# Two buffers of scaled q and k, gathered rows by DMA, some squares off ScalarE, and the FFN in steps: a cosine-attention and mixture-of-depths kernel

## The chip, the cores and the metric

The kernel runs on one core of a Trainium2 chip. Five engines work on queues of their own: TensorE (PE, with PEld for its weight loads), VectorE (DVE), ScalarE (ACT), GpSimd (POOL) and SyncE (SP), the last of which here only issues DMAs. The metric is device time in microseconds (us). Before the change the median of three runs was 270.01 us (269.08 to 270.80).

## The reference

Two stages, the second on the output of the first. Shapes: q, k, v are (8, 12, 448, 64) float32, that is 8 batches, 12 heads, 448 tokens, 64 columns per head.

```python
# attention, for each batch and head
q_n = q / (norm(q) + 1e-6);  k_n = k / (norm(k) + 1e-6)
attn = softmax(q_n @ k_n.T / tau)          # tau = 0.1
x = concat over heads of (attn @ v)        # (8, 448, 768)
# mixture of depths, for each batch
scores = x @ w_gate                        # one number for each token
top_idx = the 128 tokens with the highest score
xe = x[top_idx]
ye = relu(xe @ w1) @ w2                    # 768 -> 1024 -> 768
out = x;  out[top_idx] = xe + sigmoid(scores[top_idx])[:, None] * ye
```

## The kernel before

**Slots.** Two heads make a pair; there are 48 pairs, six for each batch. The main loop runs over 48 slots, and slot `i` is the turn of pair `i`. In it the kernel computes the pair's scores in four pieces (`scores`, L275 and L280; three pieces hold both heads' 128 keys, the fourth, "piece 3", the 64 keys left over of each head), takes their exponentials on ACT (`exps`, L288 and L291), and multiplies the exponentials of the pair before by the values (`pv_tails` L304, `pv` L315). `pv_evac` (L331, L333) divides by the softmax sum on DVE and writes 128 columns of the batch's float32 tile `x_b`.

**What a slot prepares for later ones.** The squares of q and k of pair `i+5` are taken on ACT (`square`, L187); PE adds them up by eight matmuls with the identity (`sum_pe`, L194), DVE finishes the sum (L202), and for one or two pairs at a time (`NORMS`) ACT takes the logarithm and the exponential (L210, L211), POOL adds 1e-6 (L217) and DVE inverts (L220). POOL multiplies q and k of pair `i+2` by this (`scale`, L230, into the one tile `qkn`) and casts the values (`values`, L237). PE transposes the scaled q and k of pair `i+1` in 28 small transposes (`transposes`, L257), and DVE copies the result out of PSUM (`qkT_copy`, L263). POOL casts the new columns of `x_b` to bf16 (`half_x`, L354, tile `xh`).

**Mixture of depths.** The work for batch `b` is put into the slots after its last pair, counted from slot `s = 6*(b+1)`, by a table (`late`, `mid`, `early`, `last`) and the helpers `at` and `run`; a letter in the table names a place inside the slot. In order: `store_x` writes the whole `x_b` to `out` (two DMAs on SP, L346 and L347), `gate` computes the scores on DVE (L361), `rank_prep` (POOL, L371 to L374) and `rank_rep` (PE, L392, L396) spread them over partitions, `rank_count` (DVE, L416) counts how many tokens score higher, `pick` (L424) makes a 0/1 matrix, `select` (L433, L436 to L440) reads the row indices and gates out of it, and `gather` (L473) multiplies `xh` by the 0/1 matrix on PE, 24 matmuls for a batch, which gives the chosen rows already transposed; DVE copies them (L457). `ffn1` (L491, twice 24 matmuls) and `ffn2` (L500, twice 8 wide matmuls) follow, one call in one place of one slot each; their results are taken out of PSUM by DVE or ACT (L455, L459, L461). `scatter` (L515) is an indirect DMA from POOL that adds the rows of `oe` onto `out`.

**Order.** It is written out by hand: each engine works through its own queue in program order, and waits are on semaphores. In a slot PE's order is: score piece 0, tails, sums, `pv`, piece 3, piece 1, transposes, piece 2, and at place "B" the FFN step. Two PSUM buffers hold score pieces, and the sums of squares share the one of piece 3, so piece 1 waits for the exponential of piece 0, piece 2 for that of piece 3, and piece 0 of the next slot for that of piece 1. SP's queue holds all loads of q, k and v (`load`, L98 and L108, four groups of up to three pairs ahead) and the stores; POOL's queue holds the loads of the two weight matrices and the scatters. Every access to `out` is kept in order with the earlier ones that may overlap it; a scatter counts as touching the whole of `out`.

**The end.** After slot 47 the last batch has no later slots to hide in: x of pair 47, the gate of its last columns, rank, pick, gather, FFN and scatter follow one another, with the FFN of batch 6 between. For the last batch the chosen rows of x are read back by an indirect DMA (L711) from a copy `x_copy` that SP writes beside `out`, and the last scatter (L726) writes plainly.

Of the kernel before, what the change touches and what calls it, by code (L numbers as in the profile page):

```python
# [14 lines left out]


@with_exitstack
def kernel(
# [18 lines left out]
    P = 128  # L37
# [44 lines left out]
    NORMS = [(0, 1), (1, 2), (3, 1), (4, 1)]  # L82
    while sum(NORMS[-1]) < N:
        NORMS.append((sum(NORMS[-1]), min(2, N - sum(NORMS[-1]))))
# [56 lines left out]
    kn = const.tile([P, 2, NB7, Dh], BF16, name="qkn")  # L141
# [11 lines left out]
    tokc = const.tile([P, NS, 2], BF16)  # L153
    for half in range(2):
        for col, base, step, mult in ((0, 0, 0, 4), (1, NC * half, 1, 3)):
            nc.gpsimd.iota(tokc[half * T:half * T + T, :, col], pattern=[[step, NS]],
                           base=base, channel_multiplier=mult,
                           allow_small_or_imprecise_dtypes=True)
# [23 lines left out]
    ss_tiles, rs_tiles, sq_tiles = {}, {}, {}  # L182

    def square(p):
        gi, g = place[p]
        sq_tiles[p] = prep.tile([P, 2, NB7 * Dh], BF16, name="sq", bufs=3)
        nc.scalar.activation(  # L187
            sq_tiles[p], raw[gi % NRAW][0][:, :, g].rearrange("p a b d -> p a (b d)"),
            AF.Square)
# [8 lines left out]
    def sum_dve(p, dst):  # L198
        n, m = nplace[p]
        if m == 0:  # L200
            ss_tiles[n] = prep.tile([P, 2, 2, NB7], FP32, name="ss")
        nc.vector.tensor_reduce(  # L202
            ss_tiles[n][:, m].rearrange("p a b -> p (a b)"),
            dst.rearrange("p (n d) -> p n d", d=D8), axis=AX.X, op=ALU.add)

    def norm_a(n):
        gn = NORMS[n][1]
        rs = prep.tile([P, 2, 2, NB7], FP32, name="rs", bufs=3)
        rs_tiles[n] = rs
        nc.scalar.activation(rs[:, :gn], ss_tiles[n][:, :gn], AF.Ln)  # L210
        nc.scalar.activation(rs[:, :gn], rs[:, :gn], AF.Exp, scale=0.5)  # L211
# [7 lines left out]
    def norm_c(n):  # L219
        nc.vector.reciprocal(norm_of(n), norm_of(n))  # L220

    def scale(p, split=False):
        gi, g = place[p]
        qk = raw[gi % NRAW][0]
        n, m = nplace[p]
        rs = rs_tiles[n]
        parts = (((nc.gpsimd, 0, NC), (nc.vector, NC, NB7)) if split
                 else ((nc.gpsimd, 0, NB7),))
        for eng, b0, b1 in parts:
            eng.tensor_mul(  # L230
                kn[:, :, b0:b1], qk[:, :, g, b0:b1],
# [19 lines left out]
    def transposes(p):  # L251
        for a in range(2):
            for s in range(NB7):
                for u in range(2):
                    r = slice(u * T, u * T + T)
                    o = column(a, u, s)
                    nc.tensor.transpose(out=qkT_ps[r, o:o + T], in_=kn[r, a, s],  # L257
# [51 lines left out]
    def pv(i):  # L309
        ex = exp_tiles[i]  # L310
        vo = vo_bufs[i % NB]
        for u in range(2):
            for j in range(NS):
                for c in range(NC):
# [34 lines left out]
    def half_x(i):  # L349
        b, hp = divmod(i, HP)  # L350
        if hp == 0:
            xh_tiles[b] = xp.tile([P, NS, D], BF16, name="xh", bufs=3)
# [14 lines left out]
    def rank_prep(b, eng=nc.gpsimd):  # L367
        g = gates[b % 2]
        sg = moe.tile([P, NS, 3], BF16, name="sg")
# [58 lines left out]
    def select(b):  # L428
        sel, sg = st[b]["sel"], st[b]["sg"]
        pk = bank()  # L430
        for o, w, src in ((0, 2, tokc), (2, 3, sg)):
            for j in range(NS):
                nc.tensor.matmul(out=pk[:, o:o + w], lhsT=sel[:, j], rhs=src[:, j],  # L433
                                 start=(j == 0), stop=(j == NS - 1))
        gr = moe.tile([P, 1], FP32, name="gr")
        nc.vector.tensor_reduce(gr, pk[:, 2:5], axis=AX.X, op=ALU.add)  # L436
# [3 lines left out]
        nc.vector.tensor_scalar_add(idx, pks, float(b * S))  # L440
        st[b].update(idx=idx, gr=gr)
# [36 lines left out]


    def ffn1(b, part, eng="D", big=False, cut=0, between=None):  # L480
        xeT = st[b]["xeT"]
        h = moe.tile([P, 4, CAP], BF16, name=f"hT{part}")
        st[b].setdefault("hT", []).extend(h[:, t] for t in range(4))
        ps = bank(big)
        order = [(f, t) for t0, t1 in ((0, cut), (cut, KD)) for f in range(4)
                 for t in range(t0, t1)]
        for m, (f, t) in enumerate(order):
            fc = part * 4 + f
            if between and m == len(order) // 2:
                between()  # L490
            nc.tensor.matmul(out=ps[:, f * CAP:(f + 1) * CAP],  # L491
                             lhsT=w1_sb[:, t, fc * P:(fc + 1) * P],
                             rhs=xeT[t], start=(m == 0) if cut else (t == 0),
                             stop=(t == KD - 1), skip_group_check=bool(cut))
        evac(eng, h.rearrange("p t c -> p (t c)"), ps, AF.Relu)
# [7 lines left out]

    def ffn2_evac(b, n, ps, eng):
        if n == 0:
            st[b]["oe"] = moe.tile([P, D], FP32, name="oe")
        evac(eng, st[b]["oe"][:, n * ND:(n + 1) * ND], ps[:, :ND], AF.Copy, st[b]["gr"])

    def ffn2(b, n, eng="D", big=False):
        ps = bank(big)  # L510
        ffn2_mm(b, n, ps, 0, KF)
        ffn2_evac(b, n, ps, eng)

    def scatter(b):
# [3 lines left out]
            in_=st[b]["oe"][:CAP], in_offset=None, compute_op=ALU.add)  # L518
# [7 lines left out]
    def run(slot, where):  # L526
        for fn, args in work.pop((slot, where), []):
# [3 lines left out]
    late = dict(gate=((2, "D1"), (3, "D1"), (4, "D1"), (5, "D1")), rep=5, rank=6, select=7,  # L531
                ffn=((8, "B"), (9, "B"), (10, "B"), (11, "A")))
    mid = dict(late, ffn=((8, "B"), (9, "AA"), (9, "B"), (10, "A")))
    early = dict(gate=((2, "D1"), (3, "D1"), (3, "D1"), (4, "D1")), rep=4, rank=5,
                 select=6, ffn=((7, "B"), (8, "AA"), (8, "B"), (9, "A")))
    last = dict(gate=((1, "D1"), (2, "D1"), (2, "D1"), (3, "D1")), rep=3, rank=4,
                select=5, ffn=())
    for b in range(B - 1):
        s = HP * (b + 1)
        m = last if b == B - 2 else early if b == B - 3 else mid if b == B - 4 else late  # L540
        at(s, "P2", store_x, b)
        for j in range(NS):
            d, w = m["gate"][j]
            at(s + d, w, gate, b, j)
        at(s + m["gate"][3][0], "P1b", rank_prep, b)
        at(s + m["rep"], "B", rank_rep, b)
        for j in range(NS):
            at(s + m["rank"], ("D0", "D1", "D3", "D3")[j], rank_count, b, j)
        for j in range(NS):
            at(s + m["rank"], "D3", pick, b, j)  # L550
        at(s + m["select"], "A", select, b)
        at(s + m["select"], "C", select_b, b)
        at(s + m["select"], "B", gather, b, 0, "A" if b == B - 2 else "D")
        if b < B - 2:
            at(s + m["select"] + 1, "A", gather, b, 1)
        for (d, w), (fn, n) in zip(m["ffn"], ((ffn1, 0), (ffn1, 1), (ffn2, 0), (ffn2, 1))):
            at(s + d, w[0], fn, b, n, "A" if w == "AA" else "D")
            if fn is ffn2 and n == 1:
                at(s + d + 1, "P2", scatter, b)
    bb = B - 1  # L560
    gc = const.tile([P, NS], FP32)

    for j in range(NS):
        at(N - 1, "P2", gate, bb, j, 0, 5 * P, None, gc)
    at(N - 1, "P2", store_x, bb, None, 0, 5 * P)
    at(N - 1, "P2", store_x, bb, None, 0, 5 * P, x_copy)
    at(5, "D1", load_wg)
    at(7, "P2", load_w, w1_sb, moe_w1, kn[:, 1, 0, 0:1])
    at(10, "P2", load_w, w2_sb, moe_w2, kn[:, 1, 0, 0:1])

    SQ = {}
    for p in range(3, N):
        SQ.setdefault({3: 0, 4: 1, 5: 1, 6: 2}.get(p, p - 5), []).append(p)
# [34 lines left out]
    due = []  # L608
    for i in range(N + 1):
        live, prev, nxt = i < N, i > 0, i + 1 < N  # L610
# [6 lines left out]
        run(i, "P1")  # L617
        sq = SQ.get(i - 1, [])
        scores(i, 0)
        if prev:  # L620
            pv_tails(i - 1)
        exps(i, 0)
        for p in SQ.get(i, []) if i else []:
# [140 lines left out]
```

## Time and profile before

| | |
|---|---|
| median of three runs | 270.01 us |
| the profiled execution's own time | 268.42 us |
| its span, first to last instruction | 266.6 us |
| ACT busy | 203.3 us (76%) |
| PE busy | 225.2 us (84%) |
| DVE busy | 175.2 us (66%) |
| POOL busy | 168.3 us (63%) |
| granted TensorE clock | 0.985 |
| moved by DMA | 53.18 MB |

The time of an execution is 1.8 us longer than its span. A busy PE isn't PE at its peak, since matmuls overlap in the pipeline; what counts is whether one group of matmuls starts where the one before it lets it. The slots can be marked off by the exponential of piece 3 (L291), which each slot has once: it starts at 12.43 us in slot 0, at 62.86 us in slot 11, 68.86 us in slot 12 and 237.14 us in slot 47. The six slots from 23 to 28 take 28.4 us.

### The profile page before, as it was taken

What the parts mean: (1) busy time and instruction counts of PE and PEld (TensorE: products, weight loads), DVE (VectorE), ACT (ScalarE), POOL (GpSimd) and SP (SyncE); (2) the same over time, 40 slices, a digit from 0 to 9 for tenths busy, and PEclk for the clock granted to TensorE, in tenths of its full rate; (3) what the DMA queues carried; (4) which work ended last, traced back from release to release, by engine and by line L of the source; (5) the groups of instructions that cost most, each with busy time, mean ns of one, the idle gap of its engine ahead of it and who ended that gap; (6) DMA issues with size and microseconds to landing.
All of it is one profiled execution on the core that took longest, in us unless ns stands there. A gap on an engine that the chain in (4) does not pass through costs nothing.

```text
span 266.6 us, 10588 instructions
## 1 busy us (share of the span) xinstructions
PE 225.2 (84%) x4584; PEld 169.9 (64%) x4584; DVE 175.2 (66%) x472; ACT 203.3 (76%) x322; POOL 168.3 (63%) x234
## 2 busy tenths in 40 slices
PE   7678877586899979999899979998999899989920
PEld 6456655465678557767677757866786667757810
DVE  2424445474977778858877778678876976898401
ACT  3698999897897798888888789779878986683400
POOL 5367676979766568575966667757846885743131
PEclk9999999999999999999999999999999999999995
DMA  7999999999999974799679985999580049047861
GB/s 248 285 286 279 264 254 275 368 260 259 267 285 350 235 161 64 167 276 285 130 153 262 260 203 84 216 283 274 101 192 20 2 61 210 4 61 161 255 116 63
DMA packets 32431, 53.18 MB, mean 199 GB/s; under 512 B 2176, under 2 KB 28672, under 8 KB 31488
## 3 DMA queue, kind: packets, MB, share of 16 engines
q1 hardware_dynamic: 28976, 45.13, 63.9%
q0 software_dynamic: 2992, 6.69, 14.6%
q8 instruction: 36, 0.59, 1.0%
q10 hardware_dynamic: 416, 0.69, 0.7%
q14 instruction: 11, 0.09, 0.1%
HBM read 40.11 MB, written 15.53 MB: 209 GB/s over the span
## 4 chain that ended last, share of the span: by engine, by line
PE 35%; DMA 21%; DVE 16%; ACT 12%; issue 7%; SPq 4%; POOL 3%; POOLq 1%; ACTq 0%
DMA v_raw<-in_v_dram 11%; PE m_ps L491 7%; ACT expS L288 7%; PE m_ps L500 6%; PE sc L275 6%; PE o_ps L315 5%; DVE junk L416 4%; DVE junk L361 3%; DMA qk_raw<-in_k_dram 3%; DMA qk_raw<-in_q_dram 3%; PE sc L194 3%; ACT expS L291 3%; PE qkT_ps L257 3%; DVE xeT L457 2%; DVE x_b L333 2%
## 5 line engine op out<-in xcount | busy, mean ns | idle before, releaser
L288 ACT ACTIVATE expS<-sc 128x896 bf16<-128x896 f32 x144 | 125.3, 917 | 17.0 <-PE sc L275 16.4
L230 POOL TENSOR_TENSOR qkn<-qk_raw,rs 128x896 bf16<-128x896 f32 (+1 forms) x48 | 80.3, 1673 | 36.4 <-PE qkT_ps L257 26.3
L275 PE MATMUL sc<-qkT 64*128 64x448 bf16 x288 | 52.3, 358 | 14.8 <-DVE qkT L263 7.3
L187 ACT ACTIVATE sq<-qk_raw 128x896 bf16<-128x896 f32 x48 | 45.2, 947 | 2.1 <-DMA qk_raw<-in_k_dram 2.0
L315 PE MATMUL o_ps<-vo,expS 128*128 128x65 bf16 x1152 | 44.6, 193 | 1.5 <-issue 1.5
L315 PEld LDWEIGHTS <-expS 128*128 128x128 bf16 x1152 | 40.3, 97 | 2.1 <-issue 1.7
L275 PEld LDWEIGHTS <-qkT 64*128 64x128 bf16 x288 | 15.4, 92 | 37.3 <-issue 21.0
L263 DVE COPY qkT<-qkT_ps 128x960 bf16<-128x960 bf16 x48 | 31.3, 653 | 7.8 <-PE qkT_ps L257 6.8
L291 ACT ACTIVATE expS<-sc 128x448 bf16<-128x448 f32 x48 | 25.7, 536 | 13.3 <-PE sc L280 13.2
L333 DVE TENSOR_TENSOR x_b<-o_ps,rden 128x512 f32<-128x512 f32 x47 | 32.5, 691 | 1.6
L257 PEld LDWEIGHTS <-qkn 64*64 64x64 bf16 x1344 | 24.9, 109 | 12.9 <-issue 8.4
L257 PE MATMUL qkT_ps<-iden_b,qkn 64*64 64x64 bf16 x1344 | 30.4, 194 | 3.2 <-POOL qkn L230 2.1
L354 POOL CAST xh<-x_b 128x512 bf16<-128x512 f32 x47 | 29.7, 633 | 2.0 <-DVE gr L436 1.3
L361 DVE CUSTOM_DVE_ANT_0 junk<-x_b,wg_b 128x768 bf16<-128x768 f32 (+1 forms) x32 | 30.5, 953 | 0.5 <-DMA wg_b<-in_moe_w_gate_dram 0.3
L194 PE MATMUL sc<-sq,iden_b 128*128 128x112 bf16 x384 | 26.9, 215 | 2.4 <-ACT expS L288 2.3
L202 DVE TENSOR_REDUCE ss<-sc 128x14 f32<-128x112 f32 x48 | 12.8, 273 | 24.4 <-PE sc L194 24.0
L237 POOL CAST vo<-v_raw 128x448 bf16<-128x448 f32 x48 | 26.8, 557 | 0.8 <-DMA v_raw<-in_v_dram 0.7
L217 POOL TENSOR_SCALAR rs<-rs 128x28 f32<-128x28 f32 (+1 forms) x26 | 8.0, 307 | 25.8 <-ACT rs L211 21.7
L491 PEld LDWEIGHTS <-w_sb 128*128 128x128 bf16 x384 | 22.2, 98 | 3.3 <-issue 3.1
L194 PEld LDWEIGHTS <-iden_b 128*128 128x128 bf16 x384 | 20.8, 98 | 4.6 <-issue 1.7
L416 DVE SCALAR_TENSOR_TENSOR junk<-m_ps,own,tie 128x448 bf16<-128x448 f32 (+1 forms) x28 | 19.0, 678 | 0.5
L491 PE MATMUL m_ps<-xeT,w_sb 128*128 128x128 bf16 x288 | 18.1, 219 | 1.3 <-DVE xeT L457 1.3
(90 smaller groups left out, 275.6 us busy)
## 6 DMA issues: line engine op xcount, KB each, us to landing
qk_raw<-in_q_dram SPq DMA_DIRECT2D x15, 672.0 KB, 10.1
qk_raw<-in_k_dram SPq DMA_DIRECT2D x15, 672.0 KB, 12.0
v_raw<-in_v_dram SPq DMA_DIRECT2D x30, 192.0 KB, 9.6
out_dram<-x_b SPq DMA_DIRECT2D x7, 768.0 KB, 7.8
v_raw<-in_v_dram SPq DMA_DIRECT2D x30, 144.0 KB, 9.0
out_dram<-x_b SPq DMA_DIRECT2D x7, 576.0 KB, 4.7
w_sb<-in_moe_w_dram POOLq DMA_DIRECT2D x2, 1536.0 KB, 18.9
out_dram<-x_b SPq DMA_DIRECT2D x1, 640.0 KB, 6.7
```

Of the source, the lines that this page charges most:

```text
L187: nc.scalar.activation(sq_tiles[p], raw[gi % NRAW][0][:, :, g].rearrange("p a b d -> p a (b d)"), AF.Square)
L194: nc.tensor.matmul(out=dst, lhsT=iden_b, rhs=sq[:, :, s * D8:(s + 1) * D8], start=(s == 0), stop=(s == Dh // D8 - 1))
L230: eng.tensor_mul(kn[:, :, b0:b1], qk[:, :, g, b0:b1], rs[:, m, :, b0:b1].rearrange("p a (b o) -> p a b o", o=1) .to_broadcast([P, 2, b1 - ...
L257: nc.tensor.transpose(out=qkT_ps[r, o:o + T], in_=kn[r, a, s], identity=iden_b[r, r], tile_position=(u * T, u * T))
L263: nc.vector.tensor_copy(qkT_tiles[p], qkT_ps[:, :W])
L275: nc.tensor.matmul(out=sc[:, u, :S], lhsT=qkT[r, KO + c * P:KO + (c + 1) * P], rhs=qkT[r, :S], start=True, stop=True, tile_position=(u * D ...
L288: nc.scalar.activation(ex[:, 2 * c:2 * c + 2], sc[:, :, :S], AF.Exp, scale=inv_tau)
L291: nc.scalar.activation(ex[:, TAIL], sc[:, 0, :S], AF.Exp, scale=inv_tau)
L315: nc.tensor.matmul(out=o_ps[:, u, j * E:(j + 1) * E], lhsT=ex[:, 2 * c + u, qc(j)], rhs=vo[:, u * NS + c], start=False, stop=(c == NC - 1) ...
L333: nc.vector.tensor_mul(dst.rearrange("p j (u d) -> p j u d", u=2), o[:, :, :, :Dh], rden.to_broadcast([P, NS, 2, Dh]))
L361: nc.vector.tensor_tensor_reduce(out=junk[:, d0:d1], in0=src, in1=wg_b[:, d0:d1], scale=1.0, scalar=0.0 if prev is None else prev[:, j:j + 1],
L491: nc.tensor.matmul(out=ps[:, f * CAP:(f + 1) * CAP], lhsT=w1_sb[:, t, fc * P:(fc + 1) * P], rhs=xeT[t], start=(m == 0) if cut else (t == 0 ...
```

## The change

It does these things at once.

1. **Two tiles of scaled q and k** (`kns`, by the parity of the pair) in place of one.
2. **Squares.** 28 of the 48 pairs leave ACT: 17 are squared on POOL, 11 on DVE (`SQUARES_ON`). Norms are taken for groups of one to three pairs (`GROUP`), 24 groups for 26.
3. **Rows by DMA.** For batches 0 to 5 the bf16 copy `half_x` and the matmuls of `gather` fall away. `fetch` reads the 128 chosen rows back from `out` by an indirect DMA on POOL, `half_xs` casts them on POOL, and `turn` transposes them on PE (six transposes) with one copy on DVE. The fetched rows also serve as the addend: `ffn2_evac` adds x on DVE, and `scatter` writes plainly. Batch 6 keeps the old way.
4. **select** reads gates and token numbers from one tile `gtok`, in four matmuls for eight.
5. **FFN in steps.** `ffn1` and `ffn2` take a range of their contraction steps; `PLANS` holds for each batch the slot and place of each step. For batches 0 to 2, `fetch` comes two slots after the store, `scatter` 11 slots after it.
6. **Order in the slot.** `ORDER` (and `ORDER_FIRST` for slots 0 and 1) lists the pieces of a slot; `step` runs them. The tails come before piece 0, `pv` is cut in two by head, and there are places (X0, A0, X1) between.
7. **Stores and loads.** `store_x` of batches 0 to 6 moves later by one to five slots; the first 640 columns of the last batch are stored in five parts in slots 43 to 47, as its pairs end. The weights are loaded one and four slots later.
8. **The end.** Part of `pv` and of batch 6's `gather` moves into slot 47; one gate product of the last batch goes to POOL and ACT; the scatter of batch 6 now stands behind the last batch's `select`; the scatter of batch 5 stands in slot 47.

```diff
+ORDER = ("P1 tails S0 D0 SQ sums PV0 D1 X0 A0 PV1 E0 norms P1b EV S3 S1 A T "
+         "scale S2 E3 E1 copy P2 C X1 D3 E2 B ").split()
+PLANS = [{'gate': ['2D1', '3D0', '4D1', '5D1'],
+  'prep': '5P1b', 'rank': ['6D0', '6D1', '6D0', '6D3'], 'pick': '7D0',
+  'fetch': '7P1b', 'half': '9P2', 'scatter': '16P1b', 'store': '5P1',
+  'pe': [['rep', '5X1'], ['select', '7A0'], ['turn', '10B'], ['f10:0-2', '11A0'],
+         ['f10:2-6', '11A0'], ['f11:0-3', '13X1'], ['f11:3-6', '13B'], ['f20', '14B'],
+         ['f21:0-3', '15A0'], ['f21:3-8', '15B']]},
...
+  'fetch': '8P2', 'half': '9P1b', 'scatter': '15P1b', 'store': '4P2',
...
+  'fetch': '6P2', 'half': '8P1b', 'scatter': '13P2', 'store': '3P1',
...
+  'fetch': '5P2', 'half': '6P2', 'scatter': '11P2', 'store': '1P2',
...
+LEAD = 5
+SQUARES_ON = {4: 'D', 32: 'D', 45: 'P', 1: 'P', 21: 'D', 12: 'D', 38: 'P', 40: 'P', 34: 'P', 36: 'P', 16: 'D', 22: 'P', 2: 'D', 28: 'P', 31: 'P', 5: 'P', 3: 'D', 15: 'D', 9: 'P', 10: 'D', 11: 'D', 46: 'P', 19: 'D', 8: 'P', 43: 'P', 29: 'P', 24: 'P', 26: 'P'}
...
-    kn = const.tile([P, 2, NB7, Dh], BF16, name="qkn")
+    kns = [const.tile([P, 2, NB7, Dh], BF16, name=f"qkn{n}") for n in range(2)]
...
+        if p in SQUARES_ON:
+            eng = nc.vector if SQUARES_ON[p] == "D" else nc.gpsimd
+            eng.tensor_mul(sq_tiles[p], x, x)
+        else:
+            nc.scalar.activation(sq_tiles[p], x, AF.Square)
...
     def half_x(i):
         b, hp = divmod(i, HP)
+        if b < B - 2:
+            return
...
+    def fetch(b):
+        xs = moe.tile([P, D], FP32, name="xs")
+        st[b]["xs"] = xs
+        last = b == B - 1
+        nc.gpsimd.indirect_dma_start(
+            out=xs[:CAP], out_offset=None, in_=x_copy[:, :] if last else out_flat[:(b + 1) * S, :],
+            in_offset=bass.IndirectOffsetOnAxis(
+                ap=st[b]["row" if last else "idx"][:CAP, 0:1], axis=0))
+
+    def half_xs(b):
+        st[b]["xe"] = moe.tile([P, D], BF16, name="xe", bufs=1)
+        nc.gpsimd.tensor_copy(st[b]["xe"], st[b]["xs"])
+
+    def turn(b):
+        ps = bank().bitcast(BF16)
+        xe, xeT = st[b]["xe"], moe.tile([P, KD, CAP], BF16, name="xeT")
+        for t in range(KD):
+            nc.tensor.transpose(out=ps[:, t * CAP:(t + 1) * CAP],
+                                in_=xe[:, t * P:(t + 1) * P], identity=iden_b)
+        nc.vector.tensor_copy(xeT.rearrange("p t c -> p (t c)"), ps[:, :KD * CAP])
+        st[b]["xeT"] = [xeT[:, t] for t in range(KD)]
...
     def ffn2_evac(b, n, ps, eng):
+        if "xs" in st[b]:
+            c = slice(n * ND, (n + 1) * ND)
+            xs = st[b]["oe"] = st[b]["xs"]
+            nc.vector.scalar_tensor_tensor(
+                out=xs[:, c], in0=ps[:, :ND], scalar=st[b]["gr"], in1=xs[:, c],
+                op0=ALU.mult, op1=ALU.add)
+            return
...
+    for hp in range(HP - 1):
+        for dst in (x_copy, None):
+            at(N - HP + 1 + hp, "P2", lambda d0=hp * P, dst=dst: store_x(
+                bb, x_tiles[bb][:, :, d0:d0 + P], d0, d0 + P, dst))
...
-    at(7, "P2", load_w, w1_sb, moe_w1, kn[:, 1, 0, 0:1])
-    at(10, "P2", load_w, w2_sb, moe_w2, kn[:, 1, 0, 0:1])
+    at(8, "P2", load_w, w1_sb, moe_w1, kns[0][:, 1, 0, 0:1])
+    at(14, "P2", load_w, w2_sb, moe_w2, kns[0][:, 1, 0, 0:1])
...
-    scatter(b)
     gather(bb, 0, "A", True)
     gather(bb, 1, "D", True)
     select(bb)
     select_b(bb)
...
+    scatter(b)
+    fetch(bb)
```

## The prediction

> **What bounds the kernel now.** I read the table of stretches first, with the span cut where the kind of work changes: slots 1 to 11, which have no FFN; slots 19 to 24, one full period of six; and all after slot 47's piece 3. Its columns are the stretch, its length, then busy time of PE, PEld, DVE, ACT and POOL, the granted clock, the DMA share and GB/s.
>
> ```profile
> 12.40:62.90 50.50, 38.30 (x883) 28.33 (x882) 24.07 (x60) 46.80 (x74) 36.82 (x45) 1.00 1.07 279
> 97.60:126.50 28.90, 27.45 (x586) 20.44 (x587) 22.59 (x60) 24.25 (x38) 19.68 (x26) 1.00 0.76 189
> 237.10:266.60 29.50, 17.01 (x229) 13.46 (x228) 12.37 (x40) 8.27 (x18) 7.32 (x12) 0.87 0.62 146
> ```
>
> ACT leads the first stretch (46.8 of 50.5 us), PE the second (27.45 of 28.9); in the last no engine does, so it is a chain. Next, the timeline of PE in slot 20 (start, duration): is the busy PE really handing over group to group?
>
> ```profile
> 112.42 0.36 PE L275 MATMUL sc<-qkT 64*128 64x448 bf16 x2
> 112.72 1.51 PE L491 MATMUL m_ps<-xeT,w_sb 128*128 128x128 bf16 x24
> 114.17 0.36 PE L275 MATMUL sc<-qkT 64*128 64x448 bf16 x2
> 114.37 0.28 PE L304 MATMUL o_ps<-vo,expS 64*128 64x65 bf16 x8
> ```
>
> Yes. Piece 0 of the next slot comes 1.45 us later for the FFN step ahead of it. Start to start gives a group's price: 24 FFN matmuls 1.45 us, so 0.06 each. Then the groups table, for what is moved:
>
> ```profile
> L187 ACT ACTIVATE sq<-qk_raw 128x896 bf16<-128x896 f32 x48 | 45.2, 947 | 2.1 <-DMA qk_raw<-in_k_dram 2.0
> L230 POOL TENSOR_TENSOR qkn<-qk_raw,rs 128x896 bf16<-128x896 f32 (+1 forms) x48 | 80.3, 1673 | 36.4 <-PE qkT_ps L257 26.3
> L354 POOL CAST xh<-x_b 128x512 bf16<-128x512 f32 x47 | 29.7, 633 | 2.0 <-DVE gr L436 1.3
> L333 DVE TENSOR_TENSOR x_b<-o_ps,rden 128x512 f32<-128x512 f32 x47 | 32.5, 691 | 1.6
> L515 POOL DMA_INDIRECT out_dram<-oe,idx x7 | 11.4, 1633 | 7.3 <-DMA x_copy<-x_last 6.3 <-issue 1.0
> ```
>
> The first row is what ACT can lose; the second shows that POOL waited 26.3 us for PE to release the one `qkn`; the last, that scatters barely waited before the end. SP's own waits, the DMA issues and the chain at the end complete it:
>
> ```profile
> SPq L346 <- DMA out_dram<-oe,idx: 94.5, 6, 24.9
> ...
> out_dram<-x_b SPq DMA_DIRECT2D x7, 768.0 KB, 7.8
> ...
> 247.81 0.59 SPq L346
> 248.45 4.37 DMA out_dram<-x_last
> ...
> 253.78 5.48 DMA out_dram<-oe,idx
> ```
>
> Stores wait for scatters (SP arrives early, so most of the 94.5 us is harmless); a store lands 7.8 us after issue; and the end is store, then scatter, then the last rows.
>
> [...] the trace has 1.69 for `qkn` (whole tile), and that is used. [...] at 57.85 us a gate product and a POOL cast start together, and the cast takes 1.42 us for a usual 0.62.
>
> **Sum, against the profiled execution's 268.4 us.**
>
> *Slots 1 to 11 (50.4 us).* Pairs 4 to 16 have their squares here; nine of 13 leave ACT, 9 x 0.84 us at pitch (0.947 less the overlap) = 7.6 off 45.8. Per slot I add up every engine's groups at pitch. The largest per slot summed 45.9 before (measured: 4.5 more); after, 43.0, or 41.1 if POOL and DVE may spread over three slots, while PE's part, 35.5, stays. Gain 3 to 5; I take 4. DMA was 1.07 busy here at 279 GB/s, so supply caps it: 18 pairs, 0.688 MB each, 12.4 MB, stand for slot 12, some 45 us, below the new arrival of about 58. The later weight loads help; their POOL issues (1.03 us each) hide in POOL's idle time, or cost 1 us each.
>
> *Slots 12 to 47 (174.3 us), PE.* A batch loses 24 gather matmuls (1.47 us) and 4 of 8 selects (0.22) and gains six transposes (0.4 at the same 0.06): 1.3 us, times six batches = -7.8 us. PE's own waiting is some 1.45 us a period of six slots, six periods, 8.7 us; steps spread between scores, and a second `qkn`, can win some of it back. Bound 0 to 8.7; I take 2, since [...] each accumulation now holds its PSUM bank over slots.
>
> *POOL.* It gains 17 squares (28.7), six casts of 768 columns (0.95 each by L354's rate, 5.7), six fetches at the old fetch's 1.02 (6.1), one product (1.9); it loses 36 `half_x` (22.8) and the accumulate in six scatters (1.63 to 1.01, 3.7): +16 us, 184 of 260, 71%. That alone is covered: two `qkn` let it run about one slot ahead. Uncovered it is its excess in slots where its sum tops PE's. The DMA waits are the danger, as a waiting POOL holds the `scale` of pair i+2 behind it, which PE's transposes of the next slot need. A fetch waits for its batch's store, a scatter for all earlier stores and fetches. Two slots (8.6 us) after the store, the fetches of batches 0 to 2 just meet its 7.8. For batch 3 the cast stands half a slot after its fetch, whose rows take 4.6 us: 2.5 us. Scatters: batch 2's one slot after batch 4's store, 2 us; batch 3's 1.5; batch 4's behind stores of its own slot, 6. That is 12 us of waiting against cover of about 2 us each time; I charge 3, with 0 to 12 as bounds.
>
> *DVE.* 11 squares, 12 us, less cheaper `xeT` copies (two, 1.08, become one near 0.55): +9, 184 of 260. Each can hold POOL 1 us; covered while POOL has 25% idle, otherwise up to 11.
>
> *At nothing:* the norm groups (24 for 26), `gtok`, and ORDER itself. Cover is that PE's and ACT's work per slot stays as long; a misplaced wait costs 0.2 us a slot, 9 us, and is in the range. Start: squares of pairs 1 and 2 on POOL and DVE in place of ACT; 0 to 1 us, taken 0.
>
> *The end (29.5 us from slot 47's piece 3).* Batch 5's scatter was at slot 46 (234.7), now in slot 47, and must wait for the stores of the last batch's columns 512 to 639 of the same slot. SP reaches those late: from slot 44 its queue waits for batch 4's scatter, itself late, then works off 14 DMAs of 0.62 us. I get: those stores issued 4.8 us after slot 47's mark, landed at +9.3, scatter landed at +15 (5.5), last store and `x_copy` issued by +17, landed +21.4, last fetch at +22.3. Before, it was at +19.0 (256.14). So +3.3 us. Behind the waiting POOL stands `xg`, the last gate product: rank, pick and FFN shift some 5 us too, ending level with the chain. Bounds -1 to +6.
>
> Sum: -4 -7.8 -2 +3 +3.3 = -7.5, so 260.9. The median of the runs is 1.6 above the profiled time: 262.
>
> **Rivals.** *Everything fits*: the spread wins 6 of PE's waiting, POOL costs nothing, the end nothing: -17.8, about 252. For it: POOL at 68% of the period; the `qkn` wait of 26 us that two tiles remove. Against: every DMA on POOL now has a store just ahead. *The gain is given back*: POOL's waits reach 10 us and DVE's hold on it adds 1: about 270. *Slower*: POOL's DMA waits break through. Place: fetches and scatters in front of `scale`. Price: a store's 7.8 us plus the scatter ahead of it on the store, 5.6, less 8.6 of distance and 2 of cover = 2.8 us on each of the nine DMAs that follow a store or scatter closely, 25 us: 262 - 3 + 25 - 6 of hidden overlap = 278. It decides from 11 us of uncovered waiting on. Against: SP and the rings are half idle there (189 GB/s, later 128). That the change does nothing isn't a rival: the matmuls are gone from the program.
>
> **Numbers.** Forecast 262: 0.55; everything fits, 252: 0.21; given back, 270: 0.10; slower, 278: 0.14. Each has a spread of some 4 us. The 80% range leaves out the better half of the second case and most of the last: 252 to 273; the forecast's own is 256 to 267. One per cent of 270, some 2.7 us, is about what a measurement of this kernel can tell from no change. Faster by more 0.74, within 0.11, slower 0.15.
>
> **What would show it.** Right: ACT busy near 180; no L473 matmuls before the end but transposes instead; the period of six slots near 27 us; piece 3 of slot 11 near 59; POOL's indirect DMAs with idle time before them; the end longer than 29.5. Wrong: POOL waiting on stores for over 15 us with PE's transposes waiting for `qkn`, or DVE squares far over 1.09 us; or an end that is shorter, if SP isn't late.

## The result: slower, and the profile after

The changed kernel takes 288.07 us (median of 4 runs, 285.91 to 290.06) against 269.54 us for the kernel before: a ratio of 1.0725, 95% interval 1.0591 to 1.0859. Ratios here leave disturbed executions out (those some per cent longer at a lower clock), so one can differ a little from the ratio of two medians, and the profiled executions of e1, e5, e6, e7 and e9 below were such ones, so their stretches and slots are up to some 2% long. The profiled execution has a span of 288.3 us.

I cut the span at the same marks as before (the exponential of piece 3): slots 1 to 11, slots 19 to 24, and all after slot 47's mark. The columns are the stretch, its length, busy time of PE, PEld, DVE, ACT and POOL, the granted clock, the DMA share and GB/s.

```profile
14.60:70.10 55.50, 42.99 (x875) 31.00 (x874) 37.93 (x67) 39.39 (x62) 40.52 (x39) 0.90 0.99 237
105.40:136.40 31.00, 27.57 (x541) 19.60 (x539) 24.86 (x58) 21.05 (x34) 24.03 (x26) 0.94 0.82 244
258.50:288.30 29.80, 18.56 (x236) 14.29 (x234) 13.28 (x43) 9.07 (x20) 9.90 (x14) 0.88 0.39 96
```

ACT lost its 7.4 us in the first stretch (39.39 for 46.80), and yet the stretch is 5.1 us longer, now with no engine near its length, and at a granted clock of 0.90 where it was 1.00. The six slots went from 28.9 to 31.0 us with PE busy as long as before (27.57 for 27.45) on 541 matmul records for 586, at a clock of 0.94. The end is 0.3 us longer, no more. By stretches the 21.7 us of span are: start +2.2, slots 1 to 11 +5.1, slots 12 to 47 +14.1 (188.4 for 174.3), end +0.3.

PE's timeline in slot 20 (start, duration) still shows an FFN step between the score pieces, but not at its old pitch: 24 matmuls take 1.72 us from start to start (113.17 to 114.89), where it was 1.45. The granted clock over these 1.72 us was 0.82; in slot 27, from 141.39 to 142.84 us, the clock was 1.00 and the same 24 took 1.45 again. So the step costs what it did; the clock differs.

```profile
112.68 0.55 PE L369 MATMUL sc<-qkT 64*128 64x448 bf16 x2
113.17 1.79 PE L608 MATMUL m_ps<-xeT,w_sb 128*128 128x128 bf16 x24
114.89 0.30 PE L398 MATMUL o_ps<-vo,expS 64*128 64x65 bf16 x8
```

Next the groups (busy, mean ns of one, then the idle time before and who ended it). First the three groups of the changed kernel's squares, then `qkn`, POOL's casts of the values, the gate products, `sel`, the evacuation and the scatters:

```profile
L281 ACT ACTIVATE sq<-qk_raw 128x896 bf16<-128x896 f32 x20 | 19.1, 953 | 2.5 <-DMA qk_raw<-in_k_dram 2.0 <-POOL vo L331 0.5
L279 POOL TENSOR_TENSOR sq<-qk_raw 128x896 bf16<-128x896 f32 x17 | 28.5, 1678 | 0.0
L279 DVE TENSOR_TENSOR sq<-qk_raw 128x896 bf16<-128x896 f32 x11 | 20.7, 1885 | 0.0
L324 POOL TENSOR_TENSOR qkn<-qk_raw,rs 128x896 bf16<-128x896 f32 x46 | 78.4, 1704 | 10.2 <-DVE rden L425 4.8 <-DVE rs L312 3.0 <-PE sc L369 0.5
L331 POOL CAST vo<-v_raw 128x448 bf16<-128x448 f32 x48 | 37.1, 774 | 0.0
L457 DVE CUSTOM_DVE_ANT_0 junk<-x_b,wg_b 128x768 bf16<-128x768 f32 x28 | 40.5, 1446 | 0.1
L520 DVE TENSOR_SCALAR sel<-iota_r,rank 128x128 bf16<-128x128 bf16 x29 | 11.8, 468 | 0.3
L427 DVE TENSOR_TENSOR x_b<-o_ps,rden 128x512 f32<-128x512 f32 x47 | 32.5, 691 | 4.2 <-DMA out_dram<-x_b 2.7
L646 POOL DMA_INDIRECT out_dram<-xs,idx x7 | 7.4, 1058 | 17.0 <-DVE xs L629 7.0 <-DMA out_dram<-x_b 4.9 <-DVE gate L457 3.8
```

The same casts and the same two DVE groups in the kernel before, where no square runs on POOL:

```profile
L237 POOL CAST vo<-v_raw 128x448 bf16<-128x448 f32 x48 | 26.8, 557 | 0.8 <-DMA v_raw<-in_v_dram 0.7
L361 DVE CUSTOM_DVE_ANT_0 junk<-x_b,wg_b 128x768 bf16<-128x768 f32 x28 | 26.9, 960 | 0.4 <-DMA wg_b<-in_moe_w_gate_dram 0.3
L424 DVE TENSOR_SCALAR sel<-iota_r,rank 128x128 bf16<-128x128 bf16 x29 | 8.6, 360 | 0.3
```

POOL's squares cost just what `qkn` costs (1678 ns for 1704), and POOL's wait for PE has gone (26.3 us before `qkn`, no longer listed). But instructions of DVE that nobody touched became longer: the gate products by 486 ns each (28 of them, 13.6 us) and `sel` by 108 ns (29, 3.1 us). The squares that are new on DVE take 1885 ns in the mean, where two of them beside which POOL stood idle (at 66.83 and 150.81 us) take 1080 each (11, 8.9 us). That is some 26 us in which DVE counts as busy beyond the times of the kernel before and 1080 ns a square. The excess is uneven: the longest gate product takes 4.90 us, the longest `sel` 4.04. The evacuation L427, which reads PSUM, still takes 691 ns (690 to 693 in all 47).

The waits (total us, times, longest) add a second matter, and the DMA issues (KB each, us to landing) its cause:

```profile
SPq L440 <- DMA out_dram<-xs,idx: 48.0, 6, 19.7
...
POOL xs L578 <- DVE x_b L427: 9.4, 2, 6.2
...
DVE x_b L427 <- DMA out_dram<-x_b: 2.7, 3, 1.1
```

```profile
out_dram<-x_b SPq DMA_DIRECT2D x7, 768.0 KB, 10.5
...
out_dram<-x_b SPq DMA_DIRECT2D x7, 576.0 KB, 13.4
```

SP waits less for scatters (48.0 us for 94.5), but now the evacuation waits for a *store* of `x_b`, which it never did before, and a store's first part lands 10.5 us after issue where it took 7.8, its second 13.4 where it took 4.7.

The chain of work that ended last (start, length, what) still has a scatter, a store and the last rows at its end, but the scatter is no longer behind the store:

```profile
265.85 1.05 POOL out_dram L646
...
272.89 2.49 DMA x_copy<-x_last
...
276.80 5.37 DMA xs<-x_copy,row
```

Finally one stretch of the timeline, slot 27, the longest of all slots (9.05 us for 4.75 before). Start, duration, instruction, and in brackets the idle time before it:

```profile
142.65 1.71 POOL L324 TENSOR_TENSOR qkn<-qk_raw,rs 128x896 bf16<-128x896 f32 x1
...
144.05 4.90 DVE L457 CUSTOM_DVE_ANT_0 junk<-x_b,wg_b 128x768 bf16<-128x768 f32 x1
144.28 0.57 POOL L331 CAST vo<-v_raw 128x448 bf16<-128x448 f32 x1
...
144.81 1.68 POOL L279 TENSOR_TENSOR sq<-qk_raw 128x896 bf16<-128x896 f32 x1
...
146.44 1.68 POOL L324 TENSOR_TENSOR qkn<-qk_raw,rs 128x896 bf16<-128x896 f32 x1
148.07 1.29 POOL L331 CAST vo<-v_raw 128x448 bf16<-128x448 f32 x1
...
149.86 0.30 PE L398 MATMUL o_ps<-vo,expS 64*128 64x65 bf16 x8 [2.54 <-DVE x_b L427]
...
150.89 0.92 ACT L382 ACTIVATE expS<-sc 128x896 bf16<-128x896 f32 x1 [3.93 <-PE sc L369]
```

POOL works from 142.65 to 149.36 without a gap. The gate product starts at 144.05, inside the first multiply, and ends at 148.95, while POOL's last cast is under way; that cast takes 1.29 us for the 0.57 of the one before it. The evacuation and the copy of `qkT` stand behind it on DVE, PE stands 2.54 us for the one, and ACT 3.93 us for PE. This is the theory that the runs below test, called "held": *POOL that works without pause holds up DVE instructions that take their inputs from SBUF, such as the gate products, the squares and `sel`*.

### The profile page after: what moved, and what is told of

Same layout as the page of the kernel before. It is cut to its first block, busy times and chain, and to the rows that moved or that the text cites. A ratio compares the mean times of both kernels' runs of the same rounds, so it can differ in the third digit from the quotient of the medians.

```text
span 288.3 us, 10292 instructions
## 1 busy us (share of the span) xinstructions
PE 234.9 (81%) x4436; PEld 170.5 (59%) x4436; DVE 208.6 (72%) x474; ACT 183.4 (64%) x291; POOL 195.9 (68%) x230
## 3 DMA queue, kind: packets, MB, share of 16 engines
q0 software_dynamic: 3088, 9.05, 12.9%
## 4 chain that ended last, share of the span: by engine, by line
PE 34%; DVE 29%; ACT 11%; issue 8%; DMA 8%; POOL 7%; SPq 1%; POOLq 1%; DVEq 0%; ACTq 0%
DVE junk L457 7%; ACT expS L382 7%; PE sc L369 6%; PE sc L286 5%; PE o_ps L409 5%; DMA out_dram<-x_b 5%; PE qkT_ps L351 5%; DVE junk L512 4%; PE m_ps L608 4%; DVE sq L279 4%; DVE sel L520 3%; DVE qkT L357 3%; PE m_ps L620 3%; DVE x_b L427 3%; PE sc L374 2%
## 5 line engine op out<-in xcount | busy, mean ns | idle before, releaser
L382 ACT ACTIVATE expS<-sc 128x896 bf16<-128x896 f32 x144 | 127.4, 917 | 24.7 <-PE sc L369 20.9
L369 PE MATMUL sc<-qkT 64*128 64x448 bf16 x288 | 55.2, 379 | 8.9 <-DVE qkT L357 7.0
L409 PE MATMUL o_ps<-vo,expS 128*128 128x65 bf16 x1152 | 49.3, 197 | 1.5 <-issue 1.3
L409 PEld LDWEIGHTS <-expS 128*128 128x128 bf16 x1152 | 44.0, 100 | 3.7 <-issue 2.8
L457 DVE CUSTOM_DVE_ANT_0 junk<-x_b,wg_b 128x768 bf16<-128x768 f32 (+1 forms) x31 | 43.4, 1399 | 0.1
L331 POOL CAST vo<-v_raw 128x448 bf16<-128x448 f32 x48 | 37.1, 774 | 0.0
L427 DVE TENSOR_TENSOR x_b<-o_ps,rden 128x512 f32<-128x512 f32 x47 | 32.5, 691 | 4.2 <-DMA out_dram<-x_b 2.7
L309 POOL TENSOR_SCALAR rs<-rs 128x28 f32<-128x28 f32 (+2 forms) x24 | 7.6, 318 | 31.6 <-ACT rs L303 26.7
L279 POOL TENSOR_TENSOR sq<-qk_raw 128x896 bf16<-128x896 f32 x17 | 28.5, 1678 | 0.0
L374 PE MATMUL sc<-qkT 128*128 128x448 bf16 x48 | 18.3, 381 | 12.0 <-DVE ss L294 12.0
L279 DVE TENSOR_TENSOR sq<-qk_raw 128x896 bf16<-128x896 f32 x11 | 20.7, 1885 | 0.0
## 6 DMA issues: line engine op xcount, KB each, us to landing
out_dram<-x_b SPq DMA_DIRECT2D x7, 768.0 KB, 10.5
out_dram<-x_b SPq DMA_DIRECT2D x7, 576.0 KB, 13.4
w_sb<-in_moe_w_dram POOLq DMA_DIRECT2D x2, 1536.0 KB, 14.1
```

Source lines behind the costliest of these rows:

```text
L279: eng.tensor_mul(sq_tiles[p], x, x)
L331: nc.gpsimd.tensor_copy(vo_bufs[p % NB][:, :, :Dh], raw[gi % NRAW][1][:, g])
L369: nc.tensor.matmul(out=sc[:, u, :S], lhsT=qkT[r, KO + c * P:KO + (c + 1) * P], rhs=qkT[r, :S], start=True, stop=True, tile_position=(u * D ...
L382: nc.scalar.activation(ex[:, 2 * c:2 * c + 2], sc[:, :, :S], AF.Exp, scale=inv_tau)
L409: nc.tensor.matmul(out=o_ps[:, u, j * E:(j + 1) * E], lhsT=ex[:, 2 * c + u, qc(j)], rhs=vo[:, u * NS + c], start=False, stop=(c == NC - 1) ...
L427: nc.vector.tensor_mul(dst.rearrange("p j (u d) -> p j u d", u=2), o[:, :, :, :Dh], rden.to_broadcast([P, NS, 2, Dh]))
```

## The experiments

All times are medians; the ratio is to the kernel before, run beside it on the same chip.

| run | what it is | us | ratio, 95% interval | slots 1-11 | slots 12-47 |
|---|---|---|---|---|---|
| before | | 269.54 | 1 | 50.4 | 174.3 |
| after | | 288.07 | 1.0725 (1.0591-1.0859) | 55.5 | 188.4 |
| e1 | after, squares on ACT | 278.61 | 1.0307 (1.0177-1.0437) | 57.4 | 179.7 |
| e2 | after, one `qkn` | 299.56 | 1.1209 (1.1132-1.1286) | 57.2 | 198.9 |
| e3 | before, squares moved, two `qkn` | 282.42 | 1.0566 (1.0494-1.0637) | 51.4 | 185.8 |
| e5 | after, stores early | 284.23 | 1.0572 (1.0492-1.0652) | 57.6 | 185.2 |
| e6 | after, squares on ACT, stores and gate weights early | 264.01 | 0.9824 (0.9747-0.9902) | 54.7 | 169.9 |
| e7 | before, two `qkn` | 270.42 | 0.9942 (0.9895-0.9990) | 52.7 | 175.4 |
| e8 | after, DVE's squares only | 276.59 | 1.0304 (1.0249-1.0358) | 55.1 | 177.3 |
| e9 | e6, DVE's squares only | 271.23 | 1.0030 (0.9987-1.0073) | 56.5 | 171.3 |
| e10 | e6, rows by matmuls | 275.03 | 1.0179 (1.0035-1.0323) | 49.7 | 181.4 |
| e11 | e6, POOL's squares only | 279.23 | 1.0417 (1.0314-1.0520) | 50.5 | 183.1 |
| e12 | e6, three early squares on POOL | 264.05 | 0.9841 (0.9757-0.9925) | 52.0 | 170.0 |

### e4: the disputed instructions by themselves

No attention and no FFN here; the kernel only runs the instructions in question on two resident tiles and writes zeros. Seven phases, with a meeting of DVE and POOL between them:

```diff
+    phases = [([], ["mul"] * 6),             # (DVE's queue, POOL's queue)
+              (["mul"] * 6, []),
+              (["mul"] * 6, ["mul"] * 8),
+              (["mul"] * 6, ["cast"] * 24),
+              (["mul"] * 6, ["mul", "cast"] * 8),
+              (["psum"] * 12, ["mul"] * 6),
+              (["sel"] * 12, ["mul"] * 6)]
```

> Not the computation: only instructions of the disputed kinds in seven phases, and zeros in 128 rows of the output. Phases: GpSimd multiplies alone; VectorE multiplies of 896 float32 from two SBUF tiles alone; the same beside eight GpSimd multiplies in a row; beside 24 GpSimd casts; beside multiply and cast in turn; VectorE copies out of PSUM beside GpSimd multiplies; VectorE comparisons of 128 bf16 columns beside GpSimd multiplies. 'Held': VectorE multiplies take 1.09 us alone, and beside GpSimd's multiplies one takes from 2.7 us (one GpSimd instruction waited for) to over 10 (the whole row); the copies out of PSUM keep their time. If 1.09 us holds in every phase, the long instructions of the kernel after have another cause.

The timeline (start, duration, number of instructions): the third phase, the fifth, and the sixth:

```profile
25.26 21.35 POOL L68 TENSOR_TENSOR p_mul<-x,y 128x896 bf16<-128x896 f32 x8
...
27.30 17.38 DVE L59 TENSOR_TENSOR d_mul<-x,y 128x896 bf16<-128x896 f32 x6
...
64.41 20.25 DVE L55 COPY hold<-hold 128x64 f32<-128x64 f32 x1 [8.24 <-POOL hold L54]
...
84.58 6.09 DVE L59 TENSOR_TENSOR d_mul<-x,y 128x896 bf16<-128x896 f32 x6
...
93.07 7.25 DVE L61 CAST d_psum<-sp 128x512 bf16<-128x512 f32 x12
```

Alone, a product takes POOL 2.03 us (six in 12.20) and DVE 1.02 (six in 6.09). Together the times fit taking turns: six of DVE's need 17.38 us, 2.9 each, near one of each alone added up (3.05), and eight of POOL's 21.35, 2.67 each. Beside nothing but casts DVE's six took 8.28 us. And beside products and casts in turn, which is POOL's pattern in this kernel, a DVE copy of 64 columns that normally takes 0.20 us stood for 20.25 us, as long as POOL had work; the products behind it ran only afterwards. Twelve `sel` beside POOL's products took 11.35 us, 1019 ns each in the mean, and ended 1.18 us after the last product. The shortest in the kernel before takes 240 ns, so I estimate from these numbers that some five stood through a product (2.1 us each) and the rest ran when POOL was done. Twelve casts out of PSUM took 7.25, 0.60 from start to start and 673 ns each in the mean, while POOL multiplied all along: no more than the 692 ns of `hT` in the kernel before, which has their size. POOL's six products beside them took 12.21 us, as alone. So the hold exists, in the direction that the prediction did not price.

### e1: no square on POOL or DVE

```diff
-SQUARES_ON = {4: 'D', 32: 'D', 45: 'P', ...}
+SQUARES_ON = {}
```

> The kernel after, with all 48 squares back on ScalarE. Theory 'held': a VectorE instruction with two SBUF inputs (gate products, squares) is held while GpSimd works through a queue without pauses; without the 17 squares GpSimd pauses again, the 11 VectorE squares (20.7 us) are gone, so the mean gate product falls from 1.45 to about 1.0 us and the time from 288 to 262-270 us. Rival 'DMA waits': GpSimd's waits before fetches and scatters (27 us of idle time) set the pace; they stay, and with ScalarE busier the time is 285-292. Rival 'order': the new order of the slot and the FFN steps are at fault; again 285-292.

278.61 us is outside both ranges: the squares' move cost some 4%, but over two fifths of the loss stayed. The gates fell to 1178 ns and `sel` to 270. What was left are single slots of 6 to 10 us, at 9, 14, 20, 27 and 32. The timeline of slot 20 (9.64 us):

```profile
114.19 0.69 DVE L427 TENSOR_TENSOR x_b<-o_ps,rden 128x512 f32<-128x512 f32 x1 [5.18 <-DMA out_dram<-x_b]
...
114.88 1.08 POOL L578 DMA_INDIRECT xs<-out_dram,idx  x1 [7.39 <-DVE x_b L427]
114.93 0.40 PE L398 MATMUL o_ps<-vo,expS 64*128 64x65 bf16 x8 [3.49 <-DVE x_b L427]
```

The tile `x_b` has two buffers, so the first evacuation of batch b+2, in slot 6(b+1)+7, overwrites what the store of batch b still reads. That store stood in slot 6(b+1) before the change and for batches 0 to 2 stands in slot 6(b+1)+5 after it (for batch 3 in +4, then earlier): some two slots, 9 to 10 us, for transfers of 10.5 and, its second part, 13.4 us in the changed kernel, and up to 12.9 us in e1. This is a second cause, "late store". At slot 9 it was the load of the gate's weights, for which the first gate product waited 4.9 us.

### e3: the squares moved in the kernel before

```diff
-    kn = const.tile([P, 2, NB7, Dh], BF16, name="qkn")
+    kns = [const.tile([P, 2, NB7, Dh], BF16, name=f"qkn{n}") for n in range(2)]
...
+        if p in SQUARES_ON:
+            eng = nc.vector if SQUARES_ON[p] == "D" else nc.gpsimd
+            eng.tensor_mul(sq_tiles[p], x, x)
```

> The kernel before, with only two parts of the change: two tiles of scaled q and k, and the 28 squares on GpSimd and VectorE. Its order, FFN and gather on TensorE stay. 'Held': gate products grow from 0.96 to 1.3 us or more and the time from 270 to 278-290, although ScalarE loses 25 us of work. 'DMA waits' and 'order': neither is here, so the relief of ScalarE shows: 260-267.

282.42 us, in the range of "held". Without ORDER, PLANS, fetch or late stores, these two parts alone cost 5.7%. ACT lost its work (182.7 us busy), POOL came to 209.9 us and the gates to 1367 ns.

### e2: one `qkn` in the changed kernel

```diff
-    kns = [const.tile([P, 2, NB7, Dh], BF16, name=f"qkn{n}") for n in range(2)]
+    kns = [const.tile([P, 2, NB7, Dh], BF16, name=f"qkn{n}") for n in range(1)] * 2
```

> The kernel after, with one tile of scaled q and k. 'Held': GpSimd waits again for the transposes before each multiply (some 25 us in all), VectorE gets in during those pauses, gate products fall to 1.1-1.2 us and the time to 278-284. 'DMA waits' and 'order': a buffer less can't help; 288-296.

In slots 0 and 1 this order scales pair i+2 before it transposes pair i+1, so with one tile pairs 1 and 2 are overwritten and computed with other data, and slots 1 and 2 take 10.1 and 9.0 us. The result, 299.56 us, is outside both ranges. POOL got 20.6 us of waits for PE back, but the gates stayed at 1462 ns. My reading is that pauses at one place in the slot don't help when the same work is then done later in one go, but the run doesn't show it; why slots 12 to 47 became 10.5 us longer than with two tiles wasn't tried further.

### e7: two `qkn` alone, in the kernel before

> The kernel before with two qkn tiles and nothing else. Theory 'held': POOL has none of the 28 us of squares, so it still pauses and VectorE isn't held; the wait of POOL's qkn for the transposes (35.5 us idle before the qkn multiplies in the kernel before) shrinks, and the time is 262-270. Rival 'two tiles let POOL run without a pause, and that alone holds VectorE': gates over 1150 ns mean and 274-282.

```diff
-    kn = const.tile([P, 2, NB7, Dh], BF16, name="qkn")
+    kns = [const.tile([P, 2, NB7, Dh], BF16, name=f"qkn{n}") for n in range(2)]
```

No change: 0.9942 (0.9895 to 0.9990). POOL's 26.3 us of waiting for PE did go (no wait of `qkn` for the transposes is left), and it was worth nothing; PE had stood only 2.1 us for `qkn` before, and stands 2.1 us now. The gates rose to 1063 ns, with two over 2 us. With e3, the squares are what costs.

### e8: DVE's squares only

```diff
+SQUARES_ON = {p: e for p, e in SQUARES_ON.items() if e == "D"}
```

> The changed kernel with the 11 squares on VectorE kept and the 17 of POOL back on ScalarE. Theory 'held': POOL loses 28 us of work, so VectorE's squares come near 1.2 us and the gates near 1.2 us (1.89 and 1.45 in the changed kernel); the time is 277-283, most of the loss of the moved squares being POOL's share. Rival 'VectorE has too much work': nothing is won by freeing POOL, 285-290, with the squares of VectorE still above 1.6 us.

276.59 us, in the range of "held": taking the 17 squares from POOL wins four points of the ratio. But DVE's own squares stayed at 1722 ns (1080 with POOL idle), where I had expected 1200: POOL's `qkn` and casts are enough to hold them.

### e5 and e6: the store back at slot 6(b+1)

e5 changes the stores alone; e6 also puts all squares on ACT and issues the gate weights' load two slots sooner.

```diff
-  'store': '5P1',          # in every plan; 4P2, 3P1, 1P2, 1P1 in later ones
+  'store': '0P2',
...
-SQUARES_ON = {4: 'D', 32: 'D', 45: 'P', ...}
+SQUARES_ON = {}                              # e6 only
...
-    at(5, "D1", load_wg)
+    at(3, "D1", load_wg)                     # e6 only
```

> The changed kernel with each batch's store of x_b put back to slot 6(b+1), right after the last evacuation of that batch, as in the kernel before. Theory 'two causes': besides the contention of POOL and VectorE, the store moved to slot 6(b+1)+5 leaves under two slots until the first evacuation of batch b+2 writes the same x_b buffer, and the store takes about 10.9 us to land; the waits POOL xs <- DVE x_b (9.4) and PE o_ps <- DVE x_b (6.6 in the changed kernel) shrink below 4 us each and slots 14 and 20 fall under 5.5 us. Expected 280-285. Rival 'contention alone': the store's place is hidden anyway, 286-290.

> All squares on ScalarE (as in the run at 278.6), and in addition the stores put back to slot 6(b+1) and the load of the gate's weights issued at slot 3 in place of 5. Theory 'two causes': what was left in the run with squares on ScalarE were slots of 6 to 10 us at 9, 14, 20, 27, 32, each with a wait for the store of x_b or, at slot 9, for wg_b; about 15 us lie in them, so 260-267, that is below the kernel before. Rival 'the waits only change their names': the same stretches are held by POOL's queue or by the matmuls, 273-279.

e5, 284.23 us, is in the range of "two causes", though its interval overlaps that of the changed kernel. The evacuation waits for no store any more and slot 14 fell from 6.43 to 4.54 us, but slot 20 did not (5.83), and PE still waited 7.7 us for the evacuation, where under 4 was expected: I take it that behind held gates (1513 ns) the store's wait mostly lay hidden.

e6 shows both causes together: 264.01 us, 1.8% *faster* than the kernel before. Against e1, whose squares also are on ACT, it is 4.7% less (0.9824 over 1.0307), and the slots at 9, 14, 20 and 32 are now 4.2, 4.5, 4.5 and 4.6 us: 5.5 us less at slot 9, where the gate's weights had been waited for, and 10.4 us less at the three with a late store. Slot 27 stays at 6.1. Its gate group:

```profile
L457 DVE CUSTOM_DVE_ANT_0 junk<-x_b,wg_b 128x768 bf16<-128x768 f32 x28 | 33.3, 1190 | 0.1
```

Two gates of 3.0 us and more are left (3.01 in slot 10, 3.08 in slot 26, just ahead of slots of 6.9 and 6.1 us), in both of which POOL has two `qkn` multiplies with only a cast between them.

### e9, e11, e12: squares put back into e6

```diff
+SQUARES_ON = {p: e for p, e in SQUARES_ON.items() if e == "D"}    # e9
+SQUARES_ON = {p: e for p, e in SQUARES_ON.items() if e == "P"}    # e11
+SQUARES_ON = {5: 'P', 8: 'P', 9: 'P'}                             # e12
```

> The kernel of the run at 264.0 (squares on ScalarE, stores early, gate weights early) with the 11 squares of VectorE put back on VectorE. Theory 'POOL holds VectorE only where it runs without a pause': POOL has the same work as at 264.0, VectorE's squares come to 1.2-1.8 us, ScalarE loses 10 us, and the time is 260-266. Rival 'any square on VectorE costs': each of the 11 is held over 1.5 us and puts the evacuation behind it late, 268-273.

> The kernel of the run at 264.0 with the 17 squares of POOL put back on POOL. Theory 'held': POOL has 28 us more without pauses, the gates come to 1.4 us or more, and the time is 274-281: most of the loss of the changed kernel is these 17 instructions. Rival 'it takes both engines' squares': ScalarE loses 16 us of work, POOL stays under 70%, 261-267.

> The kernel of the run at 264.0 (squares on ScalarE, stores early, gate weights early) with three squares alone, of pairs 5, 8 and 9, on POOL: these run before the first gate. In the run with all 17 squares of POOL, slots 1-11 took 50.5 us against 54.7, and slots 12-47 183.1 against 169.9. Theory 'a square on POOL costs where a gate or sel stands beside it and helps where none does': slots 1-11 near 51, slots 12-47 near 170, time 259-263. Rival 'slots 1-11 depend on where POOL and VectorE happen to meet (54.7 with no square on POOL, 49.7 with the gather by matmuls, also with none)': no gain, 263-268.

e11, 279.23 us: "held" was right. Seventeen instructions of 1.7 us on POOL cost 6 points, although ACT became 13 us shorter (191.0 us busy for 204.0). DVE does the same work as in e6 and is busy 14.2 us longer (191.7 for 177.5). That POOL itself came late isn't the reason: PE's transposes stand 2.5 us for `qkn`, and 2.2 in e6. `sel` came to 498 ns, and the gates show it too:

```profile
L458 DVE CUSTOM_DVE_ANT_0 junk<-x_b,wg_b 128x768 bf16<-128x768 f32 x28 | 41.7, 1490 | 0.1
```

e9, 271.23 us: my expectation missed and its rival was right. DVE's 11 squares took 1893 ns each and cost 2 points; in e8, against e1, they had cost nothing. I take it that the waits for the stores lay over them there, but no run separates this. e12, 264.05 us: the rival was right here too. Slots 1 to 11 came to 52.0 us, but the medians of the two kernels are the same.

### e10: the rows by matmuls again

The chosen rows come from 24 matmuls with `sel` a batch in place of the fetch and its six transposes; the bf16 copies of `x_b` on POOL that these read are back too.

```diff
-        if b < B - 2:                        # half_x
-            return
...
-            for what, fn in (("fetch", fetch), ("half", half_xs)):
-                d, w = place_of(m[what])
-                at(s + d, w, fn, b)
...
-            at(slot, w, turn, b)
+            at(slot - 1, "B", gather, b, 0, "D")
+            at(slot, w, gather, b, 1, "D")
```

> The kernel of the run at 264.0 with the chosen rows again gathered by matmuls with sel (as in the kernel before) in place of the fetch by DMA and its transposes, and with the bf16 copies of x_b on POOL that this needs (36 casts more). Theory 'PE sets the six-slot period', the prediction's 7.8 us for this step: 270-275, with PE's busy time up by 4-8 us and slots 12-47 about 176-180. Rival 'the fetch wins nothing, PE's saved time goes into waits for POOL and VectorE': 261-267.

275.03 us, at the edge of "PE sets the period": 3.6 points, with PE's busy time up by 5.3 us (229.5 for 224.2) and slots 12 to 47 at 181.4 us for 169.9, above the 176 to 180 expected. So the rival is out, and against these places for `gather` the fetch wins. How much of it is PE's matmuls isn't shown: the 11.5 us also hold POOL's work, up from 161.0 to 174.9 us busy (36 casts, and scatters that add, 1.65 us each for 1.06), and what my places for the two halves of `gather` cost; the run doesn't split these.

## Why the prediction was wrong, step by step

**The step that failed is DVE, with its companion in POOL.** The prediction priced one direction alone: "Each can hold POOL 1 us; covered while POOL has 25% idle". That side came about as priced: POOL's casts of the values grew from 557 to 774 ns, 10.3 us over 48, within its "up to 11". Its 12 us for 11 squares, 1.09 each, was my estimate; with POOL idle they take 1.08. It should also have asked who waits for *DVE* while POOL goes on; in the sum this stands at nothing. The excess on DVE is the 26 us worked out above, and it stands ahead of the evacuation, the copy of `qkT` and the sums, so PE and then ACT wait. e4 shows who is held: DVE's products (2.9 us for 1.02), `sel` (1019 ns in the mean, for 360 in the kernel before) and a copy from SBUF (20.25 us for 0.20, through 16 POOL instructions) are, casts out of PSUM (673 ns) aren't. The sentence "That alone is covered: two `qkn` let it run about one slot ahead" made it worse: what was taken for cover, POOL without pauses, is what holds DVE. With e6 as base, POOL's squares cost 6 points (e11), DVE's 2 (e9), both together 7.5 (e5; its gate weights are loaded at the later place, but no wait for them shows in it).

**Slots 1 to 11, -4.** The ACT side was right: 7.4 us less work for 7.6. The largest engine of a slot didn't set the time, though. Measured +5.1. Slot 10 took 6.77 us for 4.27: in it one of DVE's seven squares of this stretch stood from 60.42 us for 3.85 us beside two multiplies and two casts of POOL. Slot 11 behind it had a granted clock of 0.61 and took 5.22 us for 3.73, and slot 1 a clock of 0.51 and 7.21 us for 6.14. In other runs with this order the stretch took 49.7 to 57.6 us, at a clock of 0.97 in the three shortest (e10, e11, e12) and of 0.85 to 0.91 in the rest; what decides it among them wasn't tried.

**Slots 12 to 47, -7.8 and -2.** The place and direction were right, as e10 and e6 show: in e6, with the hold mostly out, these slots take 169.9 us, 4.4 less than before, where the sum with POOL's 3 gave -6.8. In the changed kernel the matmuls are gone too, but no gain can be seen under the loss. What spreading the steps won, the 2 of this term, no run shows by itself.

**POOL's DMA waits, +3 within 0 to 12.** POOL's idle time there is 27.5 us (10.5 before the fetches, 17.0 before the scatters), more than twice the 12 us of waiting that I had added up, but it didn't cost by the way I described: PE's transposes stood only 0.7 us for `qkn`. What it cost otherwise no run shows. What I overlooked is what the moved stores themselves hold, the buffer of `x_b`. The prediction treated a moved store only as something that fetches and scatters wait for, at 7.8 us; it took 10.5, and the next writer of its buffer wasn't on the list. e1 against e6 puts it, with the gate weights' load, at 4.7%; beside the squares, the changed kernel against e5, it is 1.5 points, with intervals that overlap.

**Rivals.** "Slower, 278" had the sign, and not the mechanism: its nine DMA waits would have shown as PE waiting for `qkn`. "DVE squares far over 1.09 us" was the sign of being wrong that came true: 1885 ns in the mean.

**The end, +3.3.** It did not show: 29.8 us for 29.5. From slot 47's mark (258.48) the stores of the last batch's columns went out by +4.4, as I had it, but such a part landed 2.3 to 2.5 us after issue, not 4.5. The scatter was issued at +7.4, last held by a gate product (3.8 us) and not by a store, and the last fetch at +18.3 where I had +22.3. **The start, 0.** It was +2.2, out of bounds: with DVE's early squares alone the first mark is at 13.84 us and with POOL's alone at 13.45 (e9, e11), against 12.05 with neither (e6). Of the moved squares only those of pairs 1 and 2 run before this mark, from 9.15 us on POOL and from 10.48 on DVE; in e6 ACT is done with both at 9.05.

**At nothing.** That ORDER itself costs nothing isn't shown. e6 keeps it and is faster than before, but with the gain of the fetched rows in it; e10 keeps it without them and is 1.8% slower than before (1.0035 to 1.0323). Whether that is ORDER, the split steps or my places for `gather` stays open.

## What to carry to other kernels

Before work goes to POOL, list the DVE instructions that will run beside it and take their inputs from SBUF (here products, comparisons and copies, up to 20.25 us for a copy of 0.20), and what stands behind them on DVE. POOL's idle share isn't room for more work where its work holds DVE up: from e6 to e11 POOL's busy share only rose from 61% to 69%, and that cost 6 points. When a store is moved, follow its source buffer to the next writer, not only its destination to the next reader. A change of many parts can lose through two of them and still hold a gain: taking the squares and the store's place back out of this one gave the fastest kernel here (264.01 us, ratio 0.9824; e12 is level with it).

## What the runs showed of the hardware that I had not expected

The hold isn't fair sharing. With products on both sides the times fit taking turns, instruction by instruction (2.9 us for DVE's, 2.67 for POOL's, against 1.02 and 2.03 alone); with a product and a cast in turn on POOL, DVE got nothing for 20.25 us. Casts alone slowed DVE from 6.09 to 8.28 us.

A stalled PE was followed by a lower clock. Slot 41 of the changed kernel has `sel` held for 4.04 us and PE busy for 3.51 of 8.34 us, with one wait of 3.87 us; in slot 42 PE then was busy throughout at a granted clock of 0.63, and its 105 matmuls took 6.75 us. In e6, without the hold, the same 105 took 4.60 at 1.00 (columns as in the first table):

```profile
219.92:228.26 8.34, 3.51 (x77) 2.31 (x75) 8.17 (x16) 3.42 (x6) 6.87 (x7) 0.89 0.00 1
228.26:235.01 6.75, 6.75 (x105) 5.21 (x103) 2.71 (x10) 4.47 (x8) 4.37 (x6) 0.63 0.21 61
```

```profile
208.49:213.09 4.60, 4.60 (x105) 3.66 (x103) 2.95 (x10) 4.17 (x8) 4.15 (x6) 1.00 0.01 4
```

Over the run the mean clock was 0.922 for the changed kernel, 0.963 for e1 and 0.985 before, and PE was busy 234.9 us with fewer matmuls than before, which had 225.2. If the stall causes the low clock, part of what it costs comes after it; that wasn't tested by itself.
